# Two loads of keys and queries issued ahead of the first scratch reading, values alone for the last four steps, and four small reorderings beside them

## The chip, the cores and the metric

One core of one Trainium2 chip runs the kernel. The metric is the device time of one execution in microseconds (us). Three timed runs of the kernel before stand at 163.98, 165.22 and 165.46 us, a median of 165.22 us.

## The reference

The first half is an mLSTM over 4 batches, 8 heads, 768 tokens and a head width of 40. The second half is a soft mixture of experts over the 3072 x 320 result.

```python
for t in range(S):                                    # 768 tokens
    m_new = max(f_gate[t] + m, i_gate[t])
    f_stab, i_stab = exp(f_gate[t] + m - m_new), exp(i_gate[t] - m_new)
    C = f_stab * C + i_stab * outer(v[t], k[t])       # 40 x 40 per head
    n = f_stab * n + i_stab * k[t]
    y[t] = sigmoid(o_gate[t]) * (C @ q[t]) / max(abs(n @ q[t]), 1)
x = y as (3072, 320)
logits = x @ phi                                      # 32 slots, 4 per expert
d = softmax over the tokens; slot_input = d.T @ x
slot_out[e] = relu(slot_input[e] @ w1[e]) @ w2[e]     # 8 experts, 320 -> 1024 -> 320
out = softmax over the slots(logits) @ slot_out
```

## The kernel before

**Steps.** The mLSTM is worked in chunks of 128 tokens. A step is one chunk of one batch, all 8 heads, so there are 24 steps (`NSTEP`); step i is chunk i // 4 of batch i % 4. A chunk needs a 128 x 128 table of decays per head. It comes from a matmul (`expo`) of two lists: `LL` and `RR` for the first chunk, and for later ones `LB` and `RB`, of which two buffers alternate by chunk. Its exponential (ScalarE, `ew`) is multiplied by the scores of keys and queries (`scores` on TensorE into `psc`, `mix` on VectorE). `pv` multiplies the result by the values into `ph`. `qc` multiplies the queries by the state `C_` into `pq`; `decay_q` (GpSimd) scales its copy `qs`. `keys` (GpSimd) scales the keys by decays, `state` multiplies them by the values into `pst`, and `carry` adds that to `C_` (in the first chunk ScalarE copies it). `pq` and `pst` take turns in one PSUM bank, tag `ps`.

**What ends a step.** `post_ops` (lines 372 to 386, VectorE) take the denominator from `ph` (value 40 of each head; the host has put 2.0 in the values' extra column): a reduce with absolute value, a `scalar_tensor_tensor` that is the clamp at 2.0, a reciprocal, and the product with the output gate `sig`. `gate` (line 388, GpSimd) multiplies by the reciprocal into `x`. `xtr` (line 400, TensorE, ScalarE copies) transposes `x` one step later, for the logits. Logits and slots are added up per group of four steps.

**Gates.** `gate_ops` (lines 191 to 218) turn the gates of a stretch of tokens into decays: seven operations (a scan for the running maximum, sums, a clamp at -104, a scan for the sum), and four that split the result into three bf16 parts in `gp`. Tokens 0 to 127 and 128 to 255 are done before the loop on VectorE. `r2` is the list of tokens 256 to 383, with its sums on GpSimd, `r3` that of tokens 384 to 767, 384 wide. `rest` and `mid` (lines 532 to 534) say in which step of the loop which of them is emitted.

**Scratch.** The bf16 parts go through a DRAM scratch `W`: `put_gates` (line 225) writes them, `get_gates` (line 231) reads them back into `RB` and `LB` with other dimensions on the partitions. The reads wait until the writes have landed.

**Loads.** All loads are issued from SyncE in the order of the program (`load`, line 81). `load_qk(i)` brings keys and queries of step i, 512 KB, into one of three buffers `KQ`; `load_kv(i)` brings its keys by token (160 KB) and its values (164 KB) into one of four buffers `KV`; `load_sig` brings the output gates. A load waits for the last reader of its buffer. In the program the transfers take turns on eight semaphores, so that a load also waits until the load eight places before it has landed. Before the loop SyncE has: gates, masks, qk 0, gates, kv 0, qk 1, output gates, kv 1, the two constant lists of `static(1)`, then `put_gates(1, 2)`, the constants, qk 2, kv 2, `get_gates(1)`, the output gates of steps 1 to 3 (`sig[0][:, 1:]`), gates; and in step 0 of the loop qk 3, kv 3, qk 4.

**Order.** Nothing is scheduled by a planner: every engine executes its instructions in the order in which the program emits them. In step i of the loop (lines 540 to 652) the order is: loads, `expo(i + 2)`, `decay_c(i)`, `scores(i + 1)`, `qc(i + 1)`, `load_qk(i + 4)`, `mid`, `keys(i + 1)`, `gate(i - 1)`, `decay_q(i + 1)`, `mix(i + 1)`, `pv(i)`, `state(i)`, `post_ops(i)` with `carry(i)` in it, `xtr(i - 1)`, `rest`.

**End.** After the loop come the last logits, the experts' first product (`up`, from `w1`), its transposes, the second product (`down`, from 16 loads of `w2`) in three column parts of 128, 128 and 64, and the combination with the slots' softmax. `gather(hf)` (ScalarE, then VectorE) moves column part hf of the second product into the operand `so` of the final matmuls; `combine` is one of these, with its copy and its store. `downs(hf, n)` emits the next n of 16 pieces of a part, each a group of matmuls into 32-row strips.

Of the kernel before, what the change touches and what calls it, by code (L numbers as in the profile page):

```python
# [7 lines left out]
F32 = mybir.dt.float32  # L8
# [3 lines left out]
ALU = mybir.AluOpType  # L12
AX = mybir.AxisListType
# [5 lines left out]
NSTEP = B * NCH  # L19
# [47 lines left out]
def kernel(ctx: ExitStack, tc: tile.TileContext, qk, kv, og, g0, g1, g2, masks, consts, cr, cl, w1, w2, *outs):  # L67
# [13 lines left out]
    def load(dst, src):  # L81
        nc.sync.dma_start(dst, src)  # L82
# [35 lines left out]
    load(gf0, g0)  # L118
    load(msk[64:128], masks)

    dum = sb.tile([P, 2], F32, name="dum")
    V.memset(dum, 0.0)
    A.activation(dum[:, 1:2], dum[:, 0:1], AF.Exp)
    wz = sb.tile([P, 512], BF16, tag="h1", name="wz")
# [4 lines left out]
    V.memset(rst, 1.0)  # L129
    V.memset(rst.rearrange("p (c t) -> p c t", t=L)[:, :, 0:1], 0.0)  # L130
    V.memset(m[:, 0:1], NEG)

    sig, ew, rl, kr, xT, qs = {}, {}, {}, {}, {}, {}
    w1_sb, w2_sb, run = {}, {}, {}
# [2 lines left out]
    def load_qk(i):  # L137
        if i < NSTEP:
            load(KQ[i % NKQ], qk[i])

    def load_kv(i):
        if i < NSTEP:
            load(KV[i % NKV], kv[i])

    def load_sig(gi, u):
        if gi < NGRP:
# [30 lines left out]
    def static(n):  # L177
        load(RB[n].rearrange("p r j t -> p (r j t)"), cr)
        load(LB[n].rearrange("p a b s -> p (a b s)"), cl)
# [114 lines left out]
    def mix(i):  # L294
        if i >= NSTEP:
            return
        V.tensor_tensor(ew[i], pscs.pop(i), ew[i], ALU.mult)  # L297
# [17 lines left out]
    def decay_q(i, e=None):  # L315
        if i < B or i >= NSTEP:
            return
        (e or G).tensor_tensor(qs[i], qs[i], dec_of(i, 0).broadcast_to([P, 4, 2, V1]), ALU.mult)  # L318
# [53 lines left out]
    def post_ops(i):  # L372
        if i < 0:
            return []
        ph = phs[i]
        den = dens[i] = sb.tile([P, H], F32, tag="den", name=f"den{i}", bufs=2)
        s1 = s1_of(i)
        ops = [
            lambda: V.tensor_reduce(den, ph[:, :, D:V1], AX.X, ALU.max, apply_absolute_value=True),
            lambda: V.scalar_tensor_tensor(den, den, 2.0, den, ALU.max, ALU.max),  # L380
            lambda: V.reciprocal(den, den),
            lambda: V.scalar_tensor_tensor(s1, s1, 1.0, ph[:, :, 0:D], ALU.add, ALU.mult),  # L382
        ]
        if B <= i < NL:
            ops.insert(0, lambda: V.tensor_tensor(ph, ph, qs[i].rearrange("p j r d -> p (j r) d"), ALU.add))  # L385
        return ops
# [130 lines left out]
    for n in range(NX):  # L517
        G.memset(X[n][:, DM:DM + 1], 1.0)
    static(1)
    expo(0)  # L520
    emit(gate_ops(L, 2 * L, V, V))
    put_gates(1, 2)
    load(cst, consts)
    load_qk(2)
    load_kv(2)
    get_gates(1)
    load(sig[0][:, 1:], og[:, 0, 1:])
    load(gf2[:, :, 0:L], g2[:, :, 0:L])
# [1 line left out]
    keys(0)  # L530
    expo(1)
    r2, r3 = gate_ops(2 * L, 3 * L, G, V), gate_ops(3 * L, S, G, G)
    rest = {1: r2[0:3], 2: r2[3:7] + r3[0:3], 3: r2[7:] + r3[3:5], 4: r3[5:6], 5: r3[6:7], 6: r3[8:9], 7: r3[10:]}
    mid = {6: r3[7:8], 7: r3[9:10]}
    run["identr"] = sb.tile([P, P], F32R, name="identr")

# [4 lines left out]
    for i in range(NSTEP - 1):  # L541
        gm, ph_ = divmod(i - 1, GRP)
        gm -= 1
        live = gm >= 0
        if i == 0:
            load_qk(3)
        load_kv(i + 3)
        if i == 2:
            static(0)
        if i == 4:  # L550
            put_gates(2, 3)
        if i == 8:
            put_gates(3, NCH)
        if i % GRP == 2 and i > 6:
            get_gates(i // GRP + 2)
        if i < len(W1N):
            load_w1(W1N[i])
        load_wave(W2N.get(i, 0))

        expo(i + 2)  # L560
        if live and ph_ == 1:
            ex_dT(gm)
        if live and ph_ == 2:
            exp_e()
        if live and ph_ == 3:
            comb_hi()
        decay_c(i)
        scores(i + 1)
        qc(i + 1)
        load_qk(i + 4)  # L570
        if i in (4, 8):
            get_gates(i // 4 + 1)
        emit(mid.get(i, []))
        if i == 0:
            load(gf2[:, :, L:], g2[:, :, L:])
        if i % GRP < 2:
            load_sig(i // GRP + 1, i % GRP)
        if i % GRP == 3:
            sigm(i // GRP + 1)
        keys(i + 1)  # L580
        gate(i - 1)
        decay_q(i + 1)
        if i == NL - 1:
            run["x23"] = sb.tile([P, DM + 1], F32, tag="dec", name="x23")
            G.memset(run["x23"][:, DM:DM + 1], 1.0)
        mix(i + 1)
        if live and ph_ == 2:
            norm_e(gm)
        if live and ph_ == 3:
            comb_lo(G)  # L590
        pv(i)
        state(i)
        if i == 0:
            A.activation(sig[0][:, 0], sig[0][:, 0], AF.Tanh, scale=0.5)
        if i == 1:
            A.activation(sig[0][:, 1:], sig[0][:, 1:], AF.Tanh, scale=0.5)  # L596
        if live and ph_ == 0 and gm:
            comb_h(gm - 1, comb_T(pmt([P, GRP, P], f"pc{gm}")))
        if live and ph_ == 0:
            pl = pmt([P, P], f"pl{gm}")  # L600
            logits_mm(gm, pl, range(GRP))
            ex_lt(gm, pl)
        if live and ph_ == 1:
            if i == NL - 1:
                pv(NL, "ps")
                psT = pp.tile([P, 2, 512], F32, tag="psc", name="psT")
                peT = pp.tile([P, 2, 512], F32, tag="pe", name="peT")
            turn_d(gm)
            xtr(i - 1)
            if i < NL - 1:  # L610
                pd = pmt([P, GRP, NS], f"pd2{gm}")
                T.transpose(pd.rearrange("p j s -> p (j s)"), run["lt"], ident)
        if live and ph_ == 2:
            psl = slots(gm)
        ops = post_ops(i)
        emit(ops, int(i >= B))
        carry(i)
        emit(ops)
        if live and ph_ == 0:
            emit(top_ops(gm, run["lt"]))  # L620
        if live and ph_ == 1 and i < NL - 1:
            emit(e0_ops(gm, pd))
        if live and ph_ == 2:
            add_slots(gm, psl)
        if i == NL - 1:
            gate(NL - 1)
            emit(post_ops(NL))
            for h0 in (0, 4):
                gate(NL, V, h0, h0 + 4)
        if not (live and ph_ == 1):  # L630
            xtr(i - 1)
        emit(rest.get(i, []))
        if i == 0:
            G.tensor_copy(run["identr"], ident)
        if i == 1:
            turn_g(1, 2)
        if i == 3:
            turn_g(2, 3)
        if i == 6:
            turn_g(3, NCH)  # L640
        if i == NL - 2:
            slT = [sb.tile([P, n, 4, 32], F32, tag=t, name=f"slT{n}") for n, t in ((2, "kr0"), (3, "kr1"))]
            hT = [sb.tile([P, 2, 2, 4, 32], F32, tag=t, name=f"hT{t}") for t in ("RB0", "RB1", "LB0", "LB1")]
            for t in slT + hT:
                G.memset(t, 0.0)
# [177 lines left out]
    combines((0, 0), (0, 1), (0, 2), (0, 3), (0, 4), (0, 5))  # L823
    downs(1, 12)
    gather(1)
    downs(2, 2)
    combines((1, 0), (1, 1), (1, 2), (1, 3))
    downs(2, 14)
    gather(2)
    combine(1, 4, by=A)  # L830
    combine(1, 5, by=V)
# [97 lines left out]
```

## Time and profile before

| | before |
|---|---|
| median of three runs | 165.22 us (163.98 to 165.46) |
| profiled execution | 163.49 us, span 161.6 us |
| TensorE busy | 150.5 us, 93% of the span |
| VectorE, ScalarE, GpSimd busy | 116.9, 83.7, 74.1 us |
| transferred | 52.14 MB, 323 GB/s over the span |
| granted TensorE clock, mean | 0.989 |

The span runs from the first to the last instruction; the execution's time has 1.9 us more around it. Busy time of TensorE is modelled at the matmuls' ends, so a full TensorE isn't one at its peak. The granted clock is a share of full speed.

### The profile page before, as it was taken

The page shows a single profiled execution, that of the slowest core. Times are in us where ns is not written, and L with a number is a line of the kernel's source. Part 1 is how long each engine was busy: PE and PEld are TensorE (multiplying, and loading weights), DVE is VectorE, ACT ScalarE, POOL GpSimd, SP SyncE. Part 2 cuts the span into 40 slices and gives each one's busy share as a digit, 9 for nine tenths or more (in the row PEclk, how much of TensorE's full clock was granted, in tenths as well). Part 3 has the DMA queues.
Part 4 walks back from the last instruction along what each step waited for, and adds up shares of the span by engine and source line. Part 5 has one row for each costly group of instructions (what it writes and reads, how often), then busy time and mean ns, then how long its engine had stood idle before and what let it go on. Part 6 is the DMA issues. An engine that isn't in the chain of part 4 may idle for free.

```text
span 161.6 us, 6620 instructions
## 1 busy us (share of the span) xinstructions
PE 150.5 (93%) x2756; PEld 118.8 (74%) x2756; DVE 116.9 (72%) x296; ACT 83.7 (52%) x172; POOL 74.1 (46%) x121
## 2 busy tenths in 40 slices
PE   6899979599999999999999999999997999999880
PEld 2488868488888888878988788888885542696650
DVE  4996449968996988899879998798767655325440
ACT  4965376365548656565576754675453411204350
POOL 4022334968773986567836687433683004000000
PEclk9999999959999999999999999999999999999999
DMA  3877999996899987899999999999999999923696
GB/s 96 254 298 220 333 338 358 397 383 236 238 327 411 339 278 269 335 386 404 407 379 359 313 335 305 389 326 274 373 419 409 416 410 417 412 84 140 251 363 226
DMA packets 18737, 52.14 MB, mean 323 GB/s; under 512 B 3112, under 2 KB 4056, under 8 KB 18708
## 3 DMA queue, kind: packets, MB, share of 16 engines
q1 hardware_dynamic: 18564, 51.47, 87.9%
q8 instruction: 21, 0.34, 0.9%
q10 hardware_dynamic: 144, 0.26, 0.4%
q14 instruction: 8, 0.07, 0.1%
HBM read 47.55 MB, written 4.18 MB: 320 GB/s over the span
## 4 chain that ended last, share of the span: by engine, by line
PE 76%; DVE 8%; DMA 5%; POOL 3%; issue 2%; ACT 2%; SPq 2%; DVEq 0%; POOLq 0%; ACTq 0%
PE psc L292 14%; PE ph L362 12%; PE pq L306 9%; PE pt L408 6%; PE phh L724 5%; PE pe L272 5%; PE pst L344 4%; DMA sig<-in_og_dram 4%; PE psT L750 3%; PE po L773 3%; PE pl L414 2%; PE peT L750 2%; SPq L82 2%; PE psl L451 2%; DMA gf<-in_g_dram 1%
## 5 line engine op out<-in xcount | busy, mean ns | idle before, releaser
L297 DVE TENSOR_TENSOR ew<-psc,ew 128x1024 f32<-128x1024 f32 x24 | 29.3, 1219 | 10.1 <-PE psc L292 9.7
L292 PE MATMUL psc<-KQ 64*128 64x128 f32 x384 | 28.9, 291 | 1.2 <-DVE sig L382 0.9
L292 PEld LDWEIGHTS psc<-KQ 64*128 64x128 f32 x384 | 24.2, 193 | 7.1 <-DVE sig L382 1.9
L362 PE MATMUL ph<-KV,ew 128*64 128x41 f32 x768 | 25.9, 228 | 0.0
L278 ACT ACTIVATE ew<-pe 128x1024 f32<-128x1024 f32 x23 | 23.6, 1025 | 4.5 <-PE pe L270 3.4
L362 PEld LDWEIGHTS ph<-KV,ew 128*64 128x64 f32 x768 | 24.6, 138 | 0.4
L318 POOL TENSOR_TENSOR qs<-qs,dec 128x328 f32<-128x328 f32 x20 | 14.9, 746 | 18.6 <-ACT qs L309 18.4
L391 POOL TENSOR_TENSOR x<-sig,den 128x320 f32<-128x320 f32 x23 | 17.2, 746 | 11.1 <-DVE sig L382 10.2
L330 POOL TENSOR_TENSOR kr<-KV,rl 128x320 f32<-128x320 f32 x20 | 15.0, 751 | 11.9 <-ACT rl L281 9.0
L409 ACT COPY xT<-pt 128x384 f32<-128x384 f32 (+1 forms) x24 | 11.3, 470 | 11.6 <-PE pt L408 10.8
L306 PE MATMUL pq<-C,KQ 128*64 128x82 f32 x320 | 16.3, 245 | 0.0
L306 PEld LDWEIGHTS pq<-C,KQ 128*64 128x64 f32 x320 | 13.0, 140 | 2.5 <-ACT rl L281 0.2
L408 PE MATMUL pt<-cst,x 128*128 128x128 f32 x72 | 12.8, 286 | 2.1 <-POOL x L391 1.6
L309 ACT COPY qs<-pq 128x328 f32<-128x328 f32 x20 | 8.7, 433 | 9.3 <-PE pq L306 9.0
L344 PE MATMUL pst<-KV,kr 128*64 128x41 f32 x160 | 13.0, 230 | 0.4 <-issue 0.4
L385 DVE TENSOR_TENSOR ph<-ph,qs 128x328 f32<-128x328 f32 x19 | 9.6, 503 | 5.2 <-PE ph L362 4.9
L408 PEld LDWEIGHTS pt<-cst,x 128*128 128x128 f32 x72 | 7.7, 141 | 6.4 <-issue 2.7
L272 PE MATMUL pe<-RB,LB 128*128 128x256 bf16 x80 | 12.2, 275 | 0.0
L324 POOL TENSOR_TENSOR C<-C,dec 104x328 f32<-104x328 f32 x16 | 11.9, 746 | 0.0
L382 DVE SCALAR_TENSOR_TENSOR sig<-sig,ph 128x320 f32<-128x320 f32 x24 | 10.6, 440 | 1.4 <-ACT sig L596 1.4
L344 PEld LDWEIGHTS pst<-KV,kr 128*64 128x64 f32 x160 | 11.0, 138 | 0.6 <-issue 0.6
L355 DVE TENSOR_TENSOR C<-pst,C 64x164 f32<-64x164 f32 (+1 forms) x32 | 10.4, 324 | 0.2
(178 smaller groups left out, 249.8 us busy)
## 6 DMA issues: line engine op xcount, KB each, us to landing
KQ<-in_qk_dram SPq DMA_DIRECT2D x24, 512.0 KB, 6.5
w<-in_w_dram SPq DMA_DIRECT2D x20, 512.0 KB, 6.3
w<-in_w_dram SPq DMA_DIRECT2D x16, 640.0 KB, 12.6
KV<-in_kv_dram SPq DMA_DIRECT2D x24, 324.0 KB, 6.3
out_dram<-ob SPq DMA_DIRECT2D x14, 256.0 KB, 2.8
sig<-in_og_dram SPq DMA_DIRECT2D x10, 320.0 KB, 6.4
RB<-in_cr_dram SPq DMA_DIRECT2D x2, 256.0 KB, 9.1
LB<-in_cl_dram SPq DMA_DIRECT2D x2, 256.0 KB, 8.0
```

What stands on the lines that cost most here:

```text
L272: T.matmul(pe[r][:, :, t0:t0 + HL], LB[c % 2][:, a, b], RB[c % 2][:, r, :, t0:t0 + HL], start=True, stop=True)
L278: A.activation(ew[i], pe_, AF.Exp)
L292: T.matmul(psc[:, r, j], t[r0:r1, 1, j], t[r0:r1, 0, j], start=True, stop=True)
L297: V.tensor_tensor(ew[i], pscs.pop(i), ew[i], ALU.mult)
L306: T.matmul(pq[64 * a:64 * a + 64, j].rearrange("p u d -> p (u d)"), t[:, 0, j, 64 * a:64 * a + 64], C_[:, b, j].rearrange("p u d -> p (u d ...
L318: (e or G).tensor_tensor(qs[i], qs[i], dec_of(i, 0).broadcast_to([P, 4, 2, V1]), ALU.mult)
L324: G.tensor_tensor(c, c, dec_of(i, 1, 104).broadcast_to([104, 4, 2, V1]), ALU.mult)
L330: G.tensor_tensor(t[:, 24:24 + DM].rearrange("p (j r d) -> p j r d", j=4, r=2), KV[i % NKV][:, 0:DM].rearrange("p (j r d) -> p j r d", j=4 ...
L344: T.matmul(pst[0:64, j], t[:, 80 * j:80 * j + 64], vc[:, 2 * j], start=True, stop=True)
L362: T.matmul(ph[64 * a:64 * a + 64, h], w[:, h % 2, h // 2, 64 * a:64 * a + 64], vc[:, h], start=i < NL or h == 0, stop=i < NL)
L391: (e or G).tensor_tensor(x_of(i)[:, h0 * D:h1 * D].rearrange("p (h d) -> p h d", d=D), s1_of(i)[:, h0:h1], dens[i][:, h0:h1].unsqueeze(2). ...
L408: T.transpose(pt[:, q, :], x[:, o:o + P], ident)
```

## The change

The keys and queries of step 2 are issued right behind the constant lists, ahead of the gate operations' scratch write in SyncE's order; those of step 3 take their old place behind the second step's values, ahead of the first reading of the scratch. For steps 20 to 23, whose keys nothing reads by token, only the values are loaded. In the gates' list `r3`, GpSimd's first two sums move from the end of step 2 to step 3, behind `decay_q`; the clamp and the third sum move from the end of step 3 to step 4, behind `mix`. The clamp of the denominator becomes a second reduce: the first one writes beside a column of 2.0, and the second takes the larger of the two. Of the last column part, four pieces instead of two go ahead of the second part's combinations.

```diff
-    dum = sb.tile([P, 2], F32, name="dum")
+    dum = sb.tile([P, H], F32, tag="den", name="dum", bufs=2)
...
+    floors = sb.tile([P, 2, H, 2], F32, name="floors")
+    floor = [floors[:, n] for n in range(2)]
+    V.memset(floors, 2.0)
...
     def load_kv(i):
         if i < NSTEP:
-            load(KV[i % NKV], kv[i])
+            k = 0 if i < NSTEP - B else DM
+            load(KV[i % NKV][:, k:], kv[i][:, k:])
...
-            lambda: V.tensor_reduce(den, ph[:, :, D:V1], AX.X, ALU.max, apply_absolute_value=True),
-            lambda: V.scalar_tensor_tensor(den, den, 2.0, den, ALU.max, ALU.max),
+            lambda: V.tensor_reduce(floor[i % 2][:, :, 0], ph[:, :, D:V1], AX.X, ALU.max, apply_absolute_value=True),
+            lambda: V.tensor_reduce(den, floor[i % 2], AX.X, ALU.max),
...
     static(1)
+    load_qk(2)
     expo(0)
     emit(gate_ops(L, 2 * L, V, V))
     put_gates(1, 2)
     load(cst, consts)
-    load_qk(2)
     load_kv(2)
+    load_qk(3)
     get_gates(1)
...
-    rest = {1: r2[0:3], 2: r2[3:7] + r3[0:3], 3: r2[7:] + r3[3:5], 4: r3[5:6], 5: r3[6:7], 6: r3[8:9], 7: r3[10:]}
+    rest = {1: r2[0:3], 2: r2[3:7] + r3[0:1], 3: r2[7:], 4: r3[5:6], 5: r3[6:7], 6: r3[8:9], 7: r3[10:]}
+    side, then = {3: r3[1:3]}, {4: r3[3:5]}
...
-        if i == 0:
-            load_qk(3)
         load_kv(i + 3)
...
         decay_q(i + 1)
+        emit(side.get(i, []))
...
         mix(i + 1)
+        emit(then.get(i, []))
...
-    downs(2, 2)
+    downs(2, 4)
     combines((1, 0), (1, 1), (1, 2), (1, 3))
-    downs(2, 14)
+    downs(2, 12)
```

## Rows read from the trace of the kernel before

**Rows 1.** The page: busy time of the engines, clock and transfer rate in 40 slices.
```profile
PE 150.5 (93%) x2756; PEld 118.8 (74%) x2756; DVE 116.9 (72%) x296; ACT 83.7 (52%) x172; POOL 74.1 (46%) x121
...
PEclk9999999959999999999999999999999999999999
...
GB/s 96 254 298 220 333 338 358 397 383 236 238 327 411 339 278 269 335 386 404 407 379 359 313 335 305 389 326 274 373 419 409 416 410 417 412 84 140 251 363 226
```

**Rows 2.** TensorE's longest wait from 36 us on: total us, times, longest.
```profile
PE po L773 <- DVE so L762: 0.7, 1, 0.7
```

**Rows 3.** The chain of waits, 14 to 25 us: start, length, what.
```profile
14.76 5.85 DMA sig<-in_og_dram
20.64 1.01 ACT sig L596
...
24.99 0.55 PE pt L408 x3
```

**Rows 4.** The chain of waits, 29 to 40 us.
```profile
30.29 0.69 POOL x L391
31.02 0.55 PE pt L408 x3
...
32.62 2.01 PE psc L292 x16
34.63 1.23 PE pq L306 x16
...
38.15 1.09 PE psc L292 x16
39.24 0.72 PE pq L306 x16
```

**Rows 5.** Timeline of TensorE, 22 to 30 us: start, length, idle before.
```profile
22.25 1.16 PE L292 MATMUL psc<-KQ 64*128 64x128 f32 x16 [0.86 <-DVE sig L382]
...
29.56 0.27 PE L345 MATMUL pst<-KV,kr 128*40 128x41 f32 x2
```

**Rows 6.** Timeline of GpSimd at the 384-wide gate sums.
```profile
27.66 1.00 POOL L199 TENSOR_TENSOR gf<-gf,m 64x384 f32<-64x384 f32 x1 [2.36 <-DVE m L198]
```

**Rows 7.** Two stretches: length, busy time of five engines, clock, DMA share, GB/s.
```profile
12.00:13.50 1.50, 1.50 (x16) 1.08 (x16) 0.69 (x1) 0.71 (x1) 0.71 (x1) 1.00 0.26 37
...
32.20:35.70 3.50, 3.50 (x36) 2.95 (x36) 2.45 (x3) 2.11 (x6) 2.78 (x4) 0.51 1.04 390
```

**Rows 8.** Timeline of SyncE: a constant list, the first scratch reading, a weight load.
```profile
5.64 0.98 SPq L82 DMA_DIRECT2D LB<-in_cl_dram  x1
...
13.92 0.38 SPq L82 DMA_DIRECT2D RB<-W  x1
...
27.36 1.11 SPq L82 DMA_DIRECT2D w<-in_w_dram  x1
```

**Rows 9.** The first scratch write, issued at 11.97 us: time to landing.
```profile
DMA to landing us min/median/max: 1.5/1.5/1.5
```

**Rows 10.** The second scratch write, issued at 32.7 us: time to landing.
```profile
DMA to landing us min/median/max: 5.9/5.9/5.9
```

**Rows 11.** Timeline of ScalarE at the second output gates.
```profile
30.84 1.27 ACT L507 ACTIVATE sig<-sig 128x1280 f32<-128x1280 f32 x1 [2.57 <-DMA sig<-in_og_dram]
```

**Rows 12.** Timeline of TensorE at step 8's decay table.
```profile
42.44 0.60 PE L272 MATMUL pe<-RB,LB 128*128 128x256 bf16 x4
```

**Rows 13.** Lines 380 and 488 alone: ns min/median/max, first and last start.
```profile
L380 DVE SCALAR_TENSOR_TENSOR den<-den x24: 166/331/935, 15.4 to 123.0; 128x8 f32<-128x8 f32 x24
...
L488 DVE TENSOR_REDUCE rsum<-e x6: 272/276/286, 51.2 to 134.8; 128x4 f32<-128x128 f32 x6
```

**Rows 14.** The chain of waits at the last step's denominator.
```profile
123.04 0.53 DVE den L380
```

**Rows 15.** Timeline of VectorE at the 384-wide clamp of the gates.
```profile
32.62 1.09 DVE L201 SCALAR_TENSOR_TENSOR gf<-gf,cst 64x384 f32<-64x384 f32 x1
```

**Rows 16.** Timeline of TensorE: the last column part behind the combinations.
```profile
153.31 1.21 PE L750 MATMUL psT<-w,hTLB 128*32 128x64 f32 x64
```

## The prediction

> **What bounds the kernel now.** The profile's page comes first. TensorE is busy for 93% of the span and its granted clock is full in every slice but one [rows 1]. Of TensorE's waits from 36 us on, none is longer than 0.7 us and none is for a transfer [rows 2]. So from there on TensorE's own work sets the time, and what VectorE, GpSimd and the transfers save is cover. Time can be won before 36 us, or in the last chain of handovers.
>
> The start is read in the chain of waits. The output gates of steps 1 to 3 decide there: issued at 14.76 us, landed 5.85 us later, then ScalarE, VectorE, a gate scan, GpSimd, and TensorE's transposes of step 1 at 24.99 [rows 3]. Ahead of that TensorE sits idle for 0.86 us before step 3's scores at 22.25 [rows 5]. The view names VectorE, but the keys and queries of step 3, issued only in step 0 of the loop, fit better: the scores need them, and nothing of VectorE's was new for them.
>
> Then GpSimd decides. The transposes of step 2 start at 31.02, behind `x` of step 2 on GpSimd, which ran from 30.29 [rows 4]. Ahead of `x` on that engine stood the keys of step 4, and ahead of these two 384-wide gate sums, of which the first had itself waited 2.36 us for a scan on VectorE [rows 6]. TensorE had ended its work at 29.56 + 0.27 = 29.83 [rows 5], so it idles 1.20 us. Behind it the clock stands at 0.51 for 3.5 us [rows 7], that is at 1.2 of 2.4 GHz: scores take 2.01 us instead of 1.09, `pq` 1.23 instead of 0.72 [rows 4].
>
> **GpSimd's sums moved (the main gain).** Keys of step 4 and `x` of step 2 no longer stand behind the two sums, of which one takes 1.00 us [rows 6], and behind the scan. The keys then wait for step 4's load, which had landed by some 27.3 (the load next in its turn goes out at 27.36 [rows 8]); two operations of 0.69 us [rows 4] end at 28.8, ahead of 29.83. The idle 1.20 us goes. What is late next is `qc` of step 5: it needs the bank that ScalarE empties behind the second output gates, whose activation starts at 30.84 and takes 1.27 us [rows 11]; with a copy that I put at 0.6 the bank is free at 32.7. TensorE would want it at 29.83 + 1.60 (from transposes to scores, 31.02 to 32.62) + 1.09 = 32.5 [rows 4]. Loads that come 1.0 to 1.5 us earlier (below) close that. The sums themselves come behind `decay_q(4)`, ahead of step 5's keys and `x`, which have about a microsecond of room before their transposes.
>
> The clamp, 1.09 us [rows 15], now stands ahead of step 4's denominators on VectorE, and the third sum in GpSimd's step 4. VectorE's results are wanted a step later, some 5.53 - 1.43 = 4.1 us at full clock (between the scores at 32.62 and 38.15 [rows 4]), so I cost them at nothing; without that cover it is 1.09 us.
>
> **The clock.** The low stretch is worth 3.5 x 0.49 = 1.7 us [rows 7]; scores and `pq` alone show 0.92 + 0.51 = 1.43 us [rows 4]. It follows on the idle time, so I take 1.65 us as gained with it, near the row that covers all of it. Bounds: 0, if it comes at another place, and 1.7.
>
> **Loads moved.** Step 2's keys and queries go out at about 6.7, when the last list's issue has ended at 5.64 + 0.98 [rows 8]. Between 12.0 and 13.5 us the transfers ran at 37 GB/s [rows 7]; 524 KB take 1.5 us at the 333 to 358 GB/s of the slices behind [rows 1], so they should fit into what stands empty. In SyncE's order they go past the scratch write, and step 3's past the scratch reading and the output gates. Between write and reading stand three loads as before: constants, values, and one of 512 KB. So the reading's issue at 13.92 [rows 8] and the output gates' landing at 20.6 stay, unless the new load is still moving when the write starts. The write took 1.5 us to land with a quiet queue [rows 9] and 5.9 us in a full one [rows 10]. I take 0.2 us more, near the first, as five microseconds lie between issue and write; bounds 0 and 1.5, the load's whole transfer. The 0.86 us [rows 5] are not won: step 3's scores start at 21.4, and TensorE waits for the transposes at 24.99 instead. All transfers behind the output gates come 1.0 to 1.5 us earlier.
>
> A rule speaks against this: the Trainium skill, DMA: Bandwidth & Descriptors, section Latency and other measured facts, says that two of the sixteen DMA engines are usually slower than the rest. No row here shows single engines. By it the quiet stretch is shorter where it counts, and I would put 0.6 us in the place of 0.2, with 2.6 us as the sum below.
>
> **Step 8's decay table.** TensorE took it at 42.44 [rows 12]. It needs the second scratch reading, which goes out when the write, issued at 32.7, has landed 5.9 us later [rows 10]: two issues of 0.38 [rows 8] end at 39.4, and 1.5 us [rows 9] make 40.9. TensorE comes 2.85 us earlier, at 39.6, the scratch 1.0 to 1.5 us earlier, at 39.4 to 39.9, or later if the reading queues behind a 512 KB load (1.5 us). A new wait of 0 to 1.8 us; I take 0.4, close to the quiet queue, since transfers had thinned out there (236 GB/s in that slice [rows 1]).
>
> **Values alone.** 4 x 164 KB less, 1.6 us of transfers at 410 GB/s [rows 1]. TensorE waits for no load there [rows 2]: gain nothing. It covers the weights' stream, which runs at 409 GB/s or more from 117 to 141 us [rows 1] and meets a TensorE that comes earlier by 2.5; without it a wait of up to 1 us.
>
> **The denominator's clamp.** It takes 166 ns alone, 331 in the median, 935 at most, while a reduce from SBUF stays at 272 to 286 in six places [rows 13]. On the path it stands once, 0.53 us at 123.04 [rows 14]. A reduce of 16 elements should take 0.17 there: gain 0.35; bounds 0.25 (at 0.28) and 0.36. Elsewhere VectorE's slack hides it. The new memset of 32 columns runs before the first gates land.
>
> **Four pieces ahead.** 64 matmuls take 1.21 us [rows 16], 16 of them 0.30. They move into TensorE's 0.7 us wait [rows 2] and leave the last chain: gain 0.27, a little under it as the ends overlap; bounds 0 and 0.3.
>
> **Sum.** 1.20 + 1.65 - 0.2 - 0.4 + 0.35 + 0.27 = 2.9 us. Against the profiled execution that is 163.49 - 2.9 = 160.6 us. That execution lies 1.7 us under the median of the runs, 165.22, about the worth of one low stretch of the clock; against the median it is 162.3. I forecast between the two, **161.3 us**, own range 159.5 to 163.0.
>
> **The rivals.**
> 1. *The low clock stays, elsewhere (0.17).* TensorE's idle before 24.99 is 0.9 us in one piece, more if the output gates land late. For it: nothing but idle time precedes the low stretch. Against: 0.86 us before 22.25 brought none. Then 1.65 is lost: 162.3 by the profiled execution, 163.0 with the same lift as the forecast's.
> 2. *The first scratch write is late, and the kernel slower (0.07).* The new load is still on its way at 11.58 and the write's small packets queue behind it. SyncE holds the reading, the output gates and all loads behind them; every microsecond goes on through the chain to 24.99. TensorE's idle grows from 0.9 to over 2.5 us there, which brings the low clock back (1.65), and step 8's table waits 1.5 us longer. For a landing 2 us late: 2.9 - 2.0 - 1.65 - 1.5 = -2.2, 165.7 us by the profiled execution. It decides from about 0.8 us on, where 2.9 - 0.8 - 1.65 is used up by step 8's wait. Against it: the transfers had run dry by 12.0 [rows 7].
> 3. *The second scratch or VectorE's longer step binds (0.12).* 1.5 us of the gain come back at step 8: 162.1 to 162.8.
> 4. *The second output gates rule as before (0.04).* `qc` of step 5 then starts no sooner than its 34.63 [rows 4] and TensorE idles in its place: with the two late terms alone, 162.9 to 164.6.
>
> **How the numbers follow.** The forecast has 0.60. The range, 159.3 to 163.8, holds most of it and of the first and third rival. 1% is about what a measurement of this kernel can tell from no change; 1% under 165.22 is 163.57. Faster: the forecast, nearly all of the first and third rival, 0.80. Same: the rest of these and the fourth, 0.13. Slower: the second, 0.07.
>
> **What would show it.** In the changed trace: step 3's scores start near 21.4; the output gates' activation still near 20.6 to 20.9; transposes of step 2 follow `pst` without a gap; the clock row has no low slice; transposes of step 3 start near 34.5; step 8's table at 39.6 to 40.2; the second reduce takes 0.17 us; the wait before the second part's combinations shrinks to 0.4. It is wrong if the first scratch reading is issued after 14.5, if the low clock comes anyway, or if TensorE waits at `pq` of step 5.

## The result, and the profile after

The changed kernel takes **161.96 us** in the median of 4 runs (161.16 to 162.23). The kernel before takes 164.60 in the median of the 4 runs beside it. The ratio is 0.9892, with a 95% interval of 0.9848 to 0.9936. Forecast was 161.3, in a range of 159.3 to 163.8. The profiled execution after takes 162.23 us with a span of 160.3. Before it took 163.49 with a span of 161.6. In the experiments each median is over all runs of a kernel, while each ratio leaves out runs that lie over 1.5% above the kernel's fastest.

The page after, with TensorE's busy time and the granted clock in 40 slices. The low slice of [rows 1] is gone:

```profile
PE 149.6 (93%) x2756; PEld 117.6 (73%) x2756; DVE 112.7 (70%) x297; ACT 83.7 (52%) x172; POOL 74.5 (46%) x121
...
PEclk9999999999999999999999999999999999999998
```

TensorE's timeline of the kernel after, 14 to 42 us, answers to [rows 4, 5, 12]. Columns: start, length, engine and line, operation, out<-in, and in brackets the idle time before it and what ended it:

```profile
21.26 1.16 PE L296 MATMUL psc<-KQ 64*128 64x128 f32 x16
...
24.33 0.55 PE L412 MATMUL pt<-cst,x 128*128 128x128 f32 x3 [0.39 <-POOL x L395]
...
28.72 0.55 PE L412 MATMUL pt<-cst,x 128*128 128x128 f32 x3
...
33.53 0.55 PE L412 MATMUL pt<-cst,x 128*128 128x128 f32 x3
...
36.07 0.82 PE L310 MATMUL pq<-C,KQ 128*64 128x82 f32 x16 [0.46 <-DVE C L359]
...
41.24 0.61 PE L276 MATMUL pe<-RB,LB 128*128 128x256 bf16 x4 [1.40 <-DMA LB<-W]
```

Step 3's scores start at 21.26, against 22.25 before. The transposes of step 1 start 0.66 us earlier, those of step 2 2.30 us earlier (31.02 to 28.72) and without a wait, those of step 3 3.64 us earlier (37.17 to 33.53). Up to here the change gives more than the sum of the prediction. Then two brackets take it back: 0.46 us at `pq` of step 6 and 1.40 us at step 8's decay table, where the lead is down to 1.20 us (42.44 to 41.24). The first costs more than its bracket: from step 3's transposes to step 4's at 39.30 it is 5.77 us, before 4.89 (37.17 to 42.06).

The chain of waits after says what made the table late. Columns: start, length, what:

```profile
29.65 2.37 DVE rem L219
...
33.02 4.17 DMA W<-gp
...
37.63 3.56 DMA LB<-W
...
41.24 0.61 PE pe L276 x4
```

The table waits for the reading of the second scratch (`LB<-W`), 3.56 us on its way. Before it stands the write with 4.17 us. It was issued at 33.02, no earlier than before (32.72), although what led up to it was earlier. It waits for four instructions on VectorE, the parts. They started 1.16 us earlier than before (28.97, not 30.13) and took 4.02 us instead of 2.56. One of them, `rem`, took 2.36 us. In the first group the same instruction on the same 64x128 elements took 0.28 us. The same stretch in VectorE's timeline of the kernel after:

```profile
29.65 2.36 DVE L219 TENSOR_TENSOR rem<-gf,gp 64x128 f32<-64x128 f32 x1
...
34.05 0.89 DVE L205 SCALAR_TENSOR_TENSOR gf<-gf,cst 64x384 f32<-64x384 f32 x1
...
35.28 0.65 DVE L359 TENSOR_TENSOR C<-pst,C 64x164 f32<-64x164 f32 x2
```

And in GpSimd's:

```profile
28.54 0.99 POOL L203 TENSOR_TENSOR gf<-gf,m 64x384 f32<-64x384 f32 x1
29.61 0.86 POOL L204 TENSOR_TENSOR gf<-gf,m 64x384 f32<-64x384 f32 x1
30.43 0.73 POOL L328 TENSOR_TENSOR C<-C,dec 104x328 f32<-104x328 f32 x1
31.13 0.73 POOL L334 TENSOR_TENSOR kr<-KV,rl 128x320 f32<-128x320 f32 x1
31.83 0.76 POOL L395 TENSOR_TENSOR x<-sig,den 128x320 f32<-128x320 f32 x1
```

GpSimd runs one operation behind the other from 28.54 to 31.83, and `rem`, which has two inputs in SBUF, lasts through three of them. The casts of the parts, with one input, stretch as well (0.22 us in the first group, 0.65 at 28.97). Before, GpSimd's row was as dense, from 27.66 to 34.98, but there VectorE's instructions with two inputs waited less:

```profile
30.41 0.71 DVE L215 TENSOR_TENSOR rem<-gf,gp 64x128 f32<-64x128 f32 x1
...
31.84 0.85 DVE L217 TENSOR_TENSOR gp<-rem,gp 64x128 bf16<-64x128 f32 x1
```

What lets an instruction in behind one GpSimd operation, and makes another wait through three, is not shown. The clamp behind it (line 205, 1.09 us in [rows 15]) takes 0.89 us and stands ahead of the carry (line 359), for which TensorE's `pq` waits.

The rest of the lead arrives at the end: 1.20 us at step 9's scores (48.90 to 47.70) and 1.25 us at ScalarE's last copy (156.99 to 155.74). In all fourteen profiles that were taken, the time between those two points is 107.6 to 108.9 us. So the edits of order, loads and scratch are judged below by what they do ahead of step 9. What stands behind it spreads as well: 108.04 us in the changed kernel, 108.92 in a second profile of it (e5).

TensorE's waits of the kernel after, from 36 us on (us in total, times, longest), answer to [rows 2]. The one at `po` has shrunk from 0.7; those at `pe` and `psa` are new:

```profile
PE pe L276 <- DMA LB<-W: 1.4, 1, 1.4
...
PE po L779 <- DVE so L768: 0.4, 1, 0.4
PE psa L708 <- DVE acc L701: 0.4, 1, 0.4
```

### The profile page after: what moved, and what is told of

Its sections match the earlier page's. It is cut to its first block, busy times and chain, and to the rows that moved or that the text cites. A ratio compares the mean times of both kernels' runs of the same rounds, so it can differ in the third digit from the quotient of the medians.

```text
span 160.3 us, 6621 instructions
## 1 busy us (share of the span) xinstructions
PE 149.6 (93%) x2756; PEld 117.6 (73%) x2756; DVE 112.7 (70%) x297; ACT 83.7 (52%) x172; POOL 74.5 (46%) x121
## 4 chain that ended last, share of the span: by engine, by line
PE 78%; DVE 7%; DMA 6%; ACT 2%; issue 2%; POOL 1%; SPq 0%; DVEq 0%; POOLq 0%; ACTq 0%
PE psc L296 14%; PE ph L366 12%; PE pq L310 8%; PE phh L730 6%; PE pt L412 5%; PE pe L276 5%; PE pe L274 4%; PE pst L348 4%; PE psT L756 3%; DMA W<-gp 3%; PE po L779 3%; PE peT L756 2%; DMA LB<-W 2%; PE pl L418 2%; PE psl L455 2%
## 5 line engine op out<-in xcount | busy, mean ns | idle before, releaser
L296 PE MATMUL psc<-KQ 64*128 64x128 f32 x384 | 27.9, 285 | 0.1
L296 PEld LDWEIGHTS psc<-KQ 64*128 64x128 f32 x384 | 23.3, 187 | 6.1 <-issue 1.9
L322 POOL TENSOR_TENSOR qs<-qs,dec 128x328 f32<-128x328 f32 x20 | 14.9, 743 | 21.3 <-ACT qs L313 20.5
```

Source lines behind the costliest of these rows:

```text
L296: T.matmul(psc[:, r, j], t[r0:r1, 1, j], t[r0:r1, 0, j], start=True, stop=True)
```

## The experiments

The runs were made in three sets (e1 to e4, e5 to e8, e9 to e12), each on another chip with the kernel before beside it (medians 164.06, 163.97 and 163.57 over 23, 29 and 36 runs). **Theory:** the order on GpSimd makes the gain, as step 2's transposes no longer wait; much of it is lost at step 8, first to the second scratch, and where that is removed to VectorE, whose instructions with two inputs in SBUF are held up beside a dense row of GpSimd's. **Rivals:** the loads issued ahead make the gain; the last column parts, the denominator's floor or the values alone make part of it; the gain is all clock.

The columns of the table: median and number of runs; ratio with its interval, and in brackets how many of the runs it rests on; how many runs had a mean granted clock of TensorE over 0.990; and, from the profiled run, the start (us) of step 2's transposes, of step 8's table and of step 9's scores.

| kernel | median (runs) | ratio, 95% (runs) | clock over 0.990 | step 2 | table | step 9 |
|---|---|---|---|---|---|---|
| before | 164.06, 163.97, 163.57 (88) | | 26 of 88 | 31.02 | 42.44 | 48.90 |
| changed | 161.96 (4) | 0.989, 0.985 to 0.994 (4) | 4 of 4 | 28.72 | 41.24 | 47.70 |
| e5, the same again | 162.51 (12) | 0.992, 0.988 to 0.996 (9) | 10 of 12 | 29.14 | 40.62 | 47.08 |
| e1, order alone | 162.11 (6) | 0.989, 0.985 to 0.993 (6) | 6 of 6 | 29.45 | 40.94 | 47.41 |
| e2, loads alone | 164.08 (12) | 0.992, 0.987 to 0.996 (5) | 3 of 12 | 31.54 | 42.99 | 49.44 |
| e3, changed without order | 162.70 (12) | 0.991, 0.987 to 0.995 (10) | 6 of 12 | 31.34 | 41.37 | 47.83 |
| e4, second write early | 162.29 (6) | 0.988, 0.982 to 0.993 (5) | 6 of 6 | 29.12 | 39.74 | 46.24 |
| e6, second reading first | 162.71 (12) | 0.994, 0.990 to 0.998 (12) | 12 of 12 | 30.19 | 41.64 | 48.09 |
| e7, e4 and e6 | 162.55 (6) | 0.989, 0.982 to 0.996 (4) | 6 of 6 | 29.26 | 41.09 | 47.73 |
| e8, two pieces | 162.31 (12) | 0.993, 0.989 to 0.996 (11) | 10 of 12 | 29.19 | 41.08 | 47.54 |
| e9, clamp behind | 162.74 (12) | 0.982, 0.976 to 0.989 (4) | 8 of 12 | 29.60 | 39.48 | 48.35 |
| e10, e9 without loads | 162.58 (12) | 0.993, 0.989 to 0.997 (8) | 10 of 12 | 30.02 | 40.64 | 47.10 |
| e11, whole values | 162.44 (12) | 0.995, 0.991 to 0.999 (12) | 11 of 12 | 29.88 | 41.67 | 48.14 |
| e12, old floor | 162.82 (12) | 0.997, 0.993 to 1.001 (10) | 10 of 12 | 29.23 | 42.51 | 48.97 |

e2's and e9's ratios rest on 5 and 4 of 12 runs; their medians over all runs lie at the level of the kernel before and of the changed kernel. By the ratios alone e1, e2 and e3 can't be told apart. What separates them is the median over all runs, and with it how many runs have the low clock.

### The order alone, and the loads alone

e1 is the kernel before with the order alone:

```diff
-    rest = {1: r2[0:3], 2: r2[3:7] + r3[0:3], 3: r2[7:] + r3[3:5], ...}
+    rest = {1: r2[0:3], 2: r2[3:7] + r3[0:1], 3: r2[7:], ...}
+    side, then = {3: r3[1:3]}, {4: r3[3:5]}
```

> The kernel before with nothing but the gates' sums, clamp and third sum moved. Theory (the order on GpSimd frees TensorE at step 2's transposes, and the gain is given back at step 8's decay table, which waits for the second scratch reading): transposes of step 2 near 29.8 instead of 31.02, no low clock behind them, transposes of step 3 near 34.5, then a wait of 1 to 2 us at step 8's table, which stays between 41.0 and 42.4 as the loads are where they were; 0.2 to 1.2 us under the kernel before. Rival (the loads made the gain): transposes of step 2 stay at 31, time as before within 0.3 us.

The median is the changed kernel's. Step 2's transposes start at 29.45 and wait for nothing themselves; a wait of 0.80 us at `pst` stands just ahead of them, and has no releaser in the profile. The table waits for the reading as in the changed kernel. The waits of e1's TensorE, 22 to 50 us:

```profile
PE pe L272 <- DMA LB<-W: 1.3, 1, 1.3
PE pst L344 <- issue: 0.8, 1, 0.8
```

e2 is the kernel before with the loads alone:

```diff
     static(1)
+    load_qk(2)
     expo(0)
...
     load(cst, consts)
-    load_qk(2)
     load_kv(2)
+    load_qk(3)
     get_gates(1)
...
-        if i == 0:
-            load_qk(3)
         load_kv(i + 3)
```

> The kernel before with nothing but the two loads of keys and queries issued earlier. Theory: step 3's scores near 21.4, but step 2's transposes still behind the two 384-wide sums, at 30 to 31, with the idle microsecond and the low clock behind it; step 8's reading 1.0 to 1.4 us earlier, which nobody waits for; within 0.7 us of the kernel before. Rival (the loads made the gain): transposes of step 2 by 29, 1.2 us or more under the kernel before.

Step 3's scores start at 21.3 as with the change, but the output gates' activation is at 21.14 (20.64 in [rows 3]), step 2's transposes wait for `x` on GpSimd at 31.54, the low slice of the clock is there, and the median is that of the kernel before. From e2's page, the clock:

```profile
PEclk9999999969999999999999999999999999999997
```

And its timeline of TensorE:

```profile
25.49 0.55 PE L408 MATMUL pt<-cst,x 128*128 128x128 f32 x3 [1.16 <-POOL x L391]
...
31.54 0.55 PE L408 MATMUL pt<-cst,x 128*128 128x128 f32 x3 [1.70 <-POOL x L391]
```

e3 is the changed kernel with e1's edit undone:

> The changed kernel with the gates' sums, clamp and third sum put back to where they were. Theory: step 2's transposes behind the sums again and the clock low behind them, so that it loses 0.8 to 1.8 us against the changed kernel and stands 0.8 to 1.8 us under the kernel before by the reduce in place of the clamp and the earlier loads. Rival (the order is worth nothing): 161.7 to 162.2, as the changed kernel.

TensorE waits 1.2 us at step 2's transposes, as before, but in the profiled run no low clock follows. Step 8's table starts at 41.37, 0.13 behind the changed kernel's. So one profile of the changed kernel and one of e3 say that the order is worth nothing at step 8; what the runs say beyond single profiles is told under the clock below. Its median, 162.70, is 0.59 us above e1's and 1.36 under the kernel before's, both on the same chip. So the order alone brings the whole gain (e1, 1.95 us), but without it the rest of the change keeps more than half of it, although the loads bring nothing alone (e2). Why e3 is 1.38 us faster than e2 is not shown: the pieces, the values and the floor, which are what it has more, were only taken out one by one (e8, e11, e12).

### The second scratch

e4 casts the second group's parts in step 2 and writes them in step 3:

```diff
-    rest = {..., 2: r2[3:7] + r3[0:1], 3: r2[7:], 4: r3[5:6], ...}
+    rest = {..., 2: r2[3:] + r3[0:1], 4: r3[5:6], ...}
-        if i == 4:
+        if i == 3:
             put_gates(2, 3)
```

> The changed kernel with the three bf16 parts of tokens 256 to 383 made at the end of step 2, ahead of the 384-wide scan, and their scratch write issued in step 3 instead of 4. Theory (the gain was given back at step 8's table, and VectorE's parts were late because GpSimd's sums blocked them): the write goes out at 27 to 28 instead of 33.0, TensorE doesn't wait at step 8's table, nor 0.46 us for step 4's state at the queries' product, and the gain is 1.3 to 2.0 us on the changed kernel, 160.0 to 160.7. Rival (behind the scratch something else binds, the loads or VectorE): the wait moves, gain under 0.5 us.

The write went out 4.8 us earlier (28.24), and the table started at 39.74, 1.5 us earlier. It still waits, 0.6 us, since both transfers now take longer between the loads. The profiled run, 160.41 us, is the fastest of six; the median, 162.29, is no gain on the changed kernel, as the rival has it. The chain of waits of e4:

```profile
28.24 5.10 DMA W<-gp
...
33.75 5.95 DMA LB<-W
...
39.74 0.61 PE pe L276 x4
```

e5 is the changed kernel itself, beside the three that follow:

> The changed kernel itself, beside the next three on one chip. Theory: as before, 161.5 to 162.3; the wait at step 8's table 1 to 1.6 us, no low clock before 40 us.

The median is 162.51, 0.2 us over what was expected. The table waits 1.2 us here too, and none of VectorE's instructions on the gates takes over 1.10 us: the parts take 2.97 us, the write goes out at 32.59, lands 4.52 us later, and the reading takes 3.02. So the wait at the table does not need the long hold of `rem`.

e6 issues the second reading ahead of the step's weights and keys and queries:

```diff
+        if i == 4:
+            get_gates(2)
         if i < len(W1N):
             load_w1(W1N[i])
...
-        if i in (4, 8):
+        if i == 8:
             get_gates(i // 4 + 1)
```

> The changed kernel with the second scratch reading ahead of step 4's weight load and step 8's keys and queries in SyncE's order. Theory (the reading queues behind 1 MB of other loads): LB lands 1.5 to 2.2 us after its issue instead of 3.56, the table waits 0 to 0.3 us instead of 1.40, 1.0 to 1.4 us under the changed kernel. Rival (the write's landing alone sets it): the reading's issue stays at 37.2 and the table gains under 0.4 us; or the held loads are missed later: as the changed kernel or slower.

e7 has the edits of e4 and e6:

> The changed kernel with the parts made early, as in the run before of that name, and the second reading ahead of the weight load and step 8's keys and queries. Theory: the reading is issued at 33 to 34 and lands by 38, TensorE doesn't wait at step 8's table; 1.5 to 2.2 us under the changed kernel, 159.8 to 160.5. Rival (another wait takes its place, for `x` of the steps before or for loads): under 1 us.

Both take the wait at the table away, and neither is faster (162.71 and 162.55, beside e5's 162.51). The wait stands at `pq` of step 6 instead, behind the carry. The wait of TensorE in e7, 22 to 50 us:

```profile
PE pq L310 <- DVE C L359: 1.5, 1, 1.5
```

And VectorE's clamp, in its timeline:

```profile
33.10 3.24 DVE L205 SCALAR_TENSOR_TENSOR gf<-gf,cst 64x384 f32<-64x384 f32 x1
```

The clamp, 0.54 us in e1, takes 3.24 us here and 2.16 in e6, and the carry stands behind it.

### The clamp behind the carry

e9 is e7 with the clamp and the third sum behind step 4's post operations:

```diff
-    rest = {..., 4: r3[5:6], ...}
-    side, then = {3: r3[1:3]}, {4: r3[3:5]}
+    rest = {..., 4: r3[3:6], ...}
+    side = {3: r3[1:3]}
...
-        emit(then.get(i, []))
```

> e7 with one move more: the clamp and the third sum of the third group's gates (64x128) are issued in step 4 behind the carry and the post operations, ahead of the group's scan, instead of ahead of that step's sigma work. If the gain of the order's move is given back by the blocked clamp that stands ahead of the carry on VectorE (e7: the clamp took 3.24 us, TensorE's pq waited 1.54 for the carry), and e7's two other edits have taken away the scratch wait, then TensorE waits under 0.5 at step 6's pq, step 8's table is under 40.2 in the profile (41.2 in the changed kernel and in e7), and the median is 160.3 to 161.3. Rival: the clamp is blocked there too, what stands behind it (scan, fourth group) is late and the scratch wait or another wait of VectorE takes the gain again: table at 40.8 to 41.4, median 162 to 162.7.

e10 is e9 with e2's edit undone:

> e9 with the keys' and queries' loads of steps 2 and 3 put back to where they are in the kernel before. If those loads, issued ahead of the first reading, only delay what is queued behind them (the output gates' activation was at 19.99 with the order's move alone and at 21.1 with the loads' move alone), the activation is at 19.7 to 20.2 and the median is 0.3 to 0.8 below e9's. If they carry part of the gain of the change, step 2's or 3's keys are late on GpSimd (a DMA wait of 0.5 or more at them) and the median is 0.3 or more above e9's. With neither, the two agree within 0.3.

In e9 `pq` waits no more and the table starts at 39.48. Then the hold falls on the next instructions: the clamp takes 1.45 us and the scan 3.46, the product `ew` comes behind them, and step 8's scores wait 2.0 us for it. For the table the theory held, for the time the rival: the median is 162.74. But four of the twelve runs took 159.60 to 161.31 us, and the profile is of one of the others (162.47), so what these four did otherwise is not shown. (The expectation calls the instructions 64x128; they are 64x384.) VectorE's timeline in e9:

```profile
35.98 1.45 DVE L205 SCALAR_TENSOR_TENSOR gf<-gf,cst 64x384 f32<-64x384 f32 x1
37.46 3.46 DVE L207 TENSOR_TENSOR_SCAN g<-rst,gf 64x384 f32<-64x384 f32 x1
40.85 1.19 DVE L301 TENSOR_TENSOR ew<-psc,ew 128x1024 f32<-128x1024 f32 x1
```

And GpSimd's beside the scan:

```profile
37.98 0.74 POOL L322 TENSOR_TENSOR qs<-qs,dec 128x328 f32<-128x328 f32 x1
38.68 0.73 POOL L328 TENSOR_TENSOR C<-C,dec 104x328 f32<-104x328 f32 x1
39.38 0.73 POOL L334 TENSOR_TENSOR kr<-KV,rl 128x320 f32<-128x320 f32 x1
```

In e10 the same two instructions take 0.60 and 1.37 us:

```profile
37.15 0.60 DVE L205 SCALAR_TENSOR_TENSOR gf<-gf,cst 64x384 f32<-64x384 f32 x1
37.78 1.37 DVE L207 TENSOR_TENSOR_SCAN g<-rst,gf 64x384 f32<-64x384 f32 x1
```

There GpSimd is the one that is held up, as its timeline shows: keys and `x`, 0.73 and 0.76 us in the changed kernel's rows, take 1.04 and 1.36:

```profile
37.30 1.04 POOL L334 TENSOR_TENSOR kr<-KV,rl 128x320 f32<-128x320 f32 x1
38.31 1.36 POOL L395 TENSOR_TENSOR x<-sig,den 128x320 f32<-128x320 f32 x1
```

Its profiled run had started step 1 late (the first transposes of TensorE at 21.69, 19.85 in the changed kernel) and still reached step 9 0.60 us ahead of the changed kernel. The medians of e9 and e10 differ by 0.16 us, so the loads are worth nothing that these runs can tell. In the two kernels with the order's move and the loads where they were, the output gates' activation is at 19.99 (e1) and 20.40 (e10, in spite of its late start); in nine with both it is at 19.98 to 21.74, in the median at 20.68.

### Pieces, values and floor

e8 leaves two pieces of the last column part ahead of the combinations, as before:

```diff
-    downs(2, 4)
+    downs(2, 2)
     combines((1, 0), (1, 1), (1, 2), (1, 3))
-    downs(2, 12)
+    downs(2, 14)
```

> The changed kernel with two pieces of the last column part ahead of the combinations again instead of four. Theory (behind the combinations TensorE waits for its instructions, so that 96 matmuls take as long as 112): the stretch from the start of the four combinations to the gather's activation stays at 3.15 to 3.2 us, time as the changed kernel within 0.1. Rival (the pieces are worth their matmuls): 0.27 us longer in that stretch and in all.

From the first combination to ScalarE's `gather` e8 takes 3.20 us and the changed kernel 3.15. TensorE's timeline in the changed kernel; the 64 matmuls are those of [rows 16]:

```profile
150.21 1.20 PE L779 MATMUL po<-cT,so 128*128 128x512 f32 x4 [0.43 <-DVE so L768]
151.34 0.65 PE L756 MATMUL psT<-w,hTRB 128*32 128x64 f32 x32
151.81 1.46 PE L756 MATMUL psT<-w,hTLB 128*32 128x64 f32 x64
153.20 2.50 PE L779 MATMUL po<-cT,so 128*128 128x512 f32 x8
```

And in e8:

```profile
149.97 1.20 PE L779 MATMUL po<-cT,so 128*128 128x512 f32 x4 [0.65 <-DVE so L768]
151.10 0.88 PE L756 MATMUL psT<-w,hTRB 128*32 128x64 f32 x48
151.79 1.29 PE L756 MATMUL psT<-w,hTLB 128*32 128x64 f32 x64
153.01 2.50 PE L779 MATMUL po<-cT,so 128*128 128x512 f32 x8
```

From the end of the combinations to the start of the next ones, 96 matmuls take about as long (151.34 to 153.20) as 112 (151.10 to 153.01). What holds them is not shown.

e11 loads keys and values whole in the last four steps:

```diff
-            k = 0 if i < NSTEP - B else DM
-            load(KV[i % NKV][:, k:], kv[i][:, k:])
+            load(KV[i % NKV], kv[i])
```

> The changed kernel with keys and values loaded whole in the last four steps too (four loads of 164 KB more bytes than the values alone, as before). The prediction costed these loads at nothing, since the queue is far ahead of the sums by then: the median is within 0.3 of the changed kernel's (162.0 to 162.8 in the runs so far) and no TensorE wait on a DMA grows by more than 0.2 behind step 18. If the spared bytes speed up what is queued behind them, it is slower by 0.3 to 1, with a DMA wait in the tail to show for it.

e12 has the old floor of the denominator:

```diff
-            lambda: V.tensor_reduce(floor[i % 2][:, :, 0], ph[:, :, D:V1], ...),
-            lambda: V.tensor_reduce(den, floor[i % 2], AX.X, ALU.max),
+            lambda: V.tensor_reduce(den, ph[:, :, D:V1], ...),
+            lambda: V.scalar_tensor_tensor(den, den, 2.0, den, ALU.max, ALU.max),
```

> The changed kernel with the denominator's floor put back (a scalar_tensor_tensor with two inputs in SBUF instead of the second reduction). The prediction gave the reduction 0.35 us, from the one in the last chain of posts that went from 0.53 to 0.18. If that is kept to the end, the median is 0.3 to 0.4 above the changed kernel's and the chain shows the 0.5 us again. If it is lost at the sums that wait for the accumulation on VectorE, as the trace after suggests (the lead was 1.52 there and 1.28 after them), the median is 0 to 0.2 above it.

e11's median is 0.07 us under e5's on another chip, and the intervals of the two ratios overlap; it has a wait of 0.5 us for weights in its tail, but so has e7 (0.4), which loads values alone. e12's median is 0.31 above e5's and 0.38 above e11's on its own chip, as the first theory has it, but here too the intervals overlap. The profiles say more; e12's late step 9 is not the floor's, as its clock is low there (below). From the last step's scores to the up-projection it takes 12.02 to 12.16 us with the old floor (before, e1, e2, e12). With the new one it takes 11.74 in e3, e4, e7, e9 and e10, and 12.09 in the changed kernel, e5, e6, e8 and e11. These five, and none of the others, show TensorE's wait of 0.4 us for `acc` (the row `psa` above). So the floor's 0.35 us reach the up-projection in half of the ten profiles that have it.

The instruction over the whole kernel (count, ns min/median/max, first and last start), in the changed kernel, as in [rows 13]:

```profile
L384 DVE TENSOR_REDUCE den<-floors x24: 169/170/171, 15.3 to 121.9; 128x8 f32<-128x16 f32 x24
```

And in e12:

```profile
L384 DVE SCALAR_TENSOR_TENSOR den<-den x24: 166/343/1150, 15.4 to 123.0; 128x8 f32<-128x8 f32 x24
```

## Why the prediction was right, and where its sum was not

The time lies 0.66 us over the forecast, and within both ranges that are named (159.3 to 163.8, and 159.5 to 163.0). The steps that were to lead to it hold up to 34 us, but for the output gates, which were early by luck. Behind it, the rival that had 0.12 (the second scratch or VectorE's longer step) came true. That the time came so near owes something to the level of the runs as well: the forecast stood 3.9 us under the 165.22 on record, the gain is 2.64 us against the kernel beside it, and 1.46 where it was measured again (e5).

Of the signs named, step 3's scores (21.26), the transposes of step 2 without a gap, the clock row, the second reduce (0.17 us) and the wait of 0.43 us came. The activation (19.98) and step 3's transposes (33.53) were earlier than named, step 8's table (41.24) later.

- **Idle time at step 2's transposes, 1.20.** Right. The eleven profiles with the order moved have these transposes at 28.72 to 30.19, the three without it at 31.02 to 31.54.
- **The clock, 1.65.** Right for the two profiles that the sum compares, too large for the kernels. The runs list a mean clock each; one stretch like that of [rows 7] takes it to 0.989 (1 - 3.5 x 0.49 / 161.6, an estimate). It is over 0.990 in 26 of 88 runs of the kernel before and in 89 of 102 runs of e1 and e4 to e12, which all have the order moved. With the order as before it is 3 of 12 (e2) and 6 of 12 (e3). So the order makes the low clock rare, and does not exclude it: the first rival holds for 13 runs of 102. e12's profiled run is one of them, its clock at 0.50 from 39 to 42 us, behind 1.50 us without work at `pq`. e7 waits as long there, and e3 1.22 us at step 2's transposes, with no low clock behind: idle time stood ahead of each low stretch that was read, but does not always bring one. Its price: 164.4 us in the median of the 62 runs of before at the lower clock and 163.2 in the other 26, 1.2 us; on two of the chips it is 1.6 and 1.7, on that of e1 to e4 nothing (164.1 either way). The share falls from 0.70 to 0.13, which is worth 0.57 x 1.2 = 0.7 us on average, an estimate over three chips. The step that failed is that the low stretch was taken as belonging to the kernel, as one profile showed it. Among runs over 0.990 alone, before has 163.2 and those ten kernels 162.4, so 0.8 us are gained without the clock. They can't be put down to the order: e2 and e3, which do without it, have 162.3 (3 runs) and 162.5 (6) there. The clock of e12's profiled run, and the wait:

```profile
PEclk9999999998799999999999999999999999999999
...
37.40 0.79 PE L310 MATMUL pq<-C,KQ 128*64 128x82 f32 x16 [1.50 <-DVE C L359]
```

- **The first scratch, -0.2.** The activation came at 19.98, 0.66 us earlier than before. Two things lie in it. The write was issued at 10.93 instead of 11.58, since VectorE's last part started at 10.62, just ahead of GpSimd's keys at 10.68; before, it started at 10.69 and took 0.87 us beside them. Eleven experiments had it at 0.28 us too, e6 alone at 0.87, with the write at 11.62. VectorE's row after:

```profile
10.62 0.28 DVE L221 TENSOR_TENSOR gp<-rem,gp 64x128 bf16<-64x128 f32 x1
```

And before:

```profile
10.69 0.87 DVE L217 TENSOR_TENSOR gp<-rem,gp 64x128 bf16<-64x128 f32 x1
```

  That is luck, and it does not make the 0.66 us by itself. The early write met loads still on their way and took 2.7 us to land, instead of 1.5 [rows 9], so that the reading went out at 13.74, only 0.18 earlier. In the nine experiments with the early write and the loads ahead it took 2.5 to 3.0 us; with the loads as before 1.5 (e1, e10); in e6, with the late write, 1.8, close to the 0.2 more of the prediction. And e5, the same kernel with its write at 10.95, has the activation at 20.60. So why the output gates were as early as 19.98 in this one profile is not shown; over the kernels the loads cost rather than gave, as the activations listed under e10 show. Of the rule of the Trainium skill on two slower DMA engines the runs say nothing, since no row shows single engines. With its 0.6 the sum is 2.5 us, and not 2.6.
- **Step 8's table, -0.4.** Wrong in size: 1.40 us there and 0.46 at `pq`. The working had the second scratch come 1.0 to 1.5 us earlier with the loads; its write went out at 33.02, 0.30 later than before, since it waits for VectorE's parts. The step that failed is that VectorE's results are wanted a step later and so cost nothing: beside GpSimd's sums the parts took 4.02 us instead of 2.56. `rem`, the clamp or the scan, whichever VectorE came to, took 2.16 to 3.46 us in the changed kernel, e6, e7, e9, e11 and e12. In the other five profiles with the order moved none took over 1.49, and in four of these the table still waits (e1 1.3 us, e4 0.6, e5 1.2, e8 1.9). There the way of the scratch, write and reading, is enough. The Trainium skill, SBUF — State Buffer, section Who interferes with whom, has the rule: a VectorE instruction with two inputs in SBUF contends with a GpSimd instruction that reads SBUF, and a reduce never does. The trace agrees: `rem` 0.28 to 2.36 us, the second reduce 169 to 171 ns in 24 places. It says that one instruction blocks the other; here one waited through several (3.24 us in e7, 3.46 in e9), and the measurement decides.
- **The denominator's floor, +0.35.** Right in size where it stands: 0.17 us in place of 0.53 on the path. In half of the ten profiles with it, the changed kernel's among them, a wait at `psa` that the kernel before does not have takes it back. VectorE starts `acc` there 0.90 us after the matmuls that feed it have started (changed kernel), elsewhere 0.55 (e4); why was not settled.
- **Four pieces, +0.27.** Nothing. The wait ahead of the combinations fell to 0.43 us as predicted, but what stands behind them does not get shorter with fewer matmuls (1.86 us for 96, 1.91 for 112).
- **Values alone, 0.** Right, as far as e11 can tell; a difference of half a microsecond would not show in its runs.

By places: up to step 3's transposes the two profiles show 3.64 us, where the first three terms make 2.65; the activation, 0.66 early instead of 0.2 late, makes 0.86 of the difference of 0.99. At step 8 they lose 2.44, where the term was 0.4; behind it they gain 0.05, where the last two terms make 0.62. That is 1.25 for the 2.9 of the sum. The lift of 0.7 us between the sum and the forecast covered 0.7 of the 1.65 us that are missing.

Not settled: what made the low clock come in one run and stay away in the next of the same kernel, what the rest of the change gains without the order (e3), and whether a version without the hold at step 8 is faster. e4's and e10's profiled runs, 160.41 and 161.21 us, are under the changed kernel's 162.23, but their medians over all runs, 162.29 and 162.58, are not.

## What to carry to other kernels

Work moved on one engine has a price on another: before it is moved on GpSimd, look which VectorE instructions with two inputs in SBUF will run beside it (here `rem`, 0.28 us alone, 2.36 beside the sums), and what stands behind them. A term that one profile shows, such as a low clock, is weighed by how many runs of the kernel have it. And a step that brings every input earlier moves the end only as far as the next transfer or engine that was not touched: read the wait there before adding it up.

## What the runs showed of the hardware

- One VectorE instruction can be held up through several GpSimd instructions in a row: a 64x384 scan took 0.94 us in the changed kernel and 3.46 in e9, a clamp of the same size 0.54 in e1 and 3.24 in e7.
- A start 70 ns earlier or later decides such a race: 0.28 us when VectorE starts at 10.62, 0.87 at 10.69, with GpSimd's instruction at 10.68 both times.
- A scratch write of small pieces and its reading took 5.10 and 5.95 us to land beside the loads (e4); the write alone took 1.5 us in a quiet queue [rows 9], 2.7 with a load of 512 KB sent ahead of it (changed kernel).
- Idle time of TensorE of the same length brought a low clock in one run and none in another: 1.50 us at `pq`, then 0.50 of the clock from 39 to 42 us (e12); 1.5 us at the same place, full clock (e7).
